# Sliding-window attention and a gated FFN on one core: two weight matrices folded, scores transposed, attention issued in steps between FFN matmuls

## Chip, core, metric

One core of one Trainium2 chip. The metric is the device time of one execution in microseconds. Seven inputs arrive in HBM in fp32, one fp32 output goes back; on the chip the matmul operands are cast to fp16.

## What is computed

```python
# q, k, v: (8 batches, 8 heads, 576 positions, 64), randn * 0.1
scores = q @ k.T / 8, kept where 0 <= i - j < 64, else -1e9
attn   = exp(scores - max); attn = attn / sum(attn)
x      = (attn @ v) as 4608 tokens x 512
# w1, w2: 512 x 1024; w3: 1024 x 1024; w_out: 1024 x 512
out    = ((x @ w1) * (x @ w2)) @ w3 @ w_out
```

## The kernel before

Attention goes over 8 batches and 4 pairs of heads (32 pairs). For a pair, 20 DMAs bring q and k in 128-row pieces and 10 bring v (L99 to L105), all from SyncE's queue (SP); GpSimd (POOL) casts them (L106 to L110); TensorE transposes q and k piece by piece (L116) and ScalarE (ACT) copies each transposed piece out of PSUM (L118). Then each head takes five blocks of 128 (last 64) queries one after the other. A block is a chain: scores for up to 192 keys with queries on the partitions (L128), the mask added by VectorE, DVE (L132), the row maximum (L138), its scaling on ACT (L140), exp with the row sum (L141), the reciprocal on DVE (L145), the division on ACT (L147), one or two transposes of the probabilities (L152, L155) with an ACT copy each (L153, L156), one or two matmuls with v (L157, L160), and an ACT copy into `xT` (L162), which holds the attention's output with the 512 features on partitions.

The FFN goes over 9 groups of 512 tokens. In each group eight column blocks of `a = x@w1` and `b = x@w2` take four matmuls each (L172, L174), ACT copies `a` (L177), DVE multiplies (L178); `g = ab@w3` takes 8x8 matmuls and eight ACT copies (L183, L185); the output takes 4x8 matmuls, four ACT copies and four DMAs (L190, L193, L194). That is 1440 matmuls of 512 columns. Weights are loaded through two fp32 staging buffers and cast by POOL (L75, L76).

The order on each engine is that of the tile scheduler, which takes priorities from the program's order; every engine issues its instructions in order. Four PSUM names (`ps_a` to `ps_d`) with two buffers each serve both parts.

## Time and profile before

| | |
|---|---|
| time, median of 3 runs | 946.75 us (946.46 to 947.27) |
| profiled execution, first to last instruction | 942.8 us |
| busy: TensorE matmul, ACT, DVE, POOL | 689.0, 642.3, 294.3, 99.2 us |
| instructions | 12002 |
| HBM read, written | 39.85 MB, 9.44 MB |

PE is TensorE's matmuls, PEld its weight loads. The profile gives, for each engine, busy time and a strip of 40 slices of the span in tenths; groups of instructions by source line with count, total and mean; the chain of work that ended last; and a timeline. A busy span of a matmul covers its pipeline, so its cost in a stream is the distance from one start to the next, not its own length.

### The profile page before, as it was taken

To read this page: it belongs to the slowest core of one execution; us is meant where nothing else is said; L and a number is where in the kernel's file an instruction comes from. 1 tells how busy PE (TensorE), PEld (TensorE's weight loads), DVE (VectorE), ACT (ScalarE), POOL (GpSimd) and SP (SyncE) were. 2 spreads that over 40 slices of the span, in tenths; PEclk is the share of its full clock that TensorE was granted. 3 is DMA by queue.
4 is the path that set the end of the run, shared out by engine and by line. 5 is a ranking of instruction groups with operands and counts; after the bars stand their busy time and mean duration, and the time that the engine had idled before them with its cause. 6 is when DMAs were issued, how large, how long until landed. Compare 5 with 4: busy or idle time off the path is not lost.

```text
span 942.8 us, 12002 instructions
## 1 busy us (share of the span) xinstructions
PE 689.0 (73%) x3104; PEld 316.8 (34%) x3104; DVE 294.3 (31%) x1033; ACT 642.3 (68%) x2613; POOL 99.2 (11%) x195
## 2 busy tenths in 40 slices
PE   0436666666666666666666666689999999999998
PEld 0212323333232332323232332334444444444443
...
ACT  0649899989998998998999999973333333333332
...
GB/s 216 209 126 61 62 60 60 59 60 61 60 57 54 50 54 47 52 55 45 52 56 51 45 55 8 0 1 12 34 46 22 23 45 34 12 46 45 1 45 45
DMA packets 138757, 50.11 MB, mean 53 GB/s; under 512 B 131008, under 2 KB 131008, under 8 KB 138688
## 3 DMA queue, kind: packets, MB, share of 16 engines
...
q8 instruction: 24, 0.39, 0.2%
...
HBM read 39.85 MB, written 9.44 MB: 52 GB/s over the span
## 4 chain that ended last, share of the span: by engine, by line
PE 46%; ACT 42%; DMA 4%; DVE 3%; issue 3%; POOL 1%; SPq 1%; ACTq 0%; POOLq 0%
PE ps_c L183 13%; ACT sc L141 11%; ACT scp L147 10%; PE ps_b L174 7%; PE ps_a L172 7%; PE ps_d L190 7%; ACT xT L162 7%; ACT at L153 4%; PE ps_a L116 4%; DMA stg<-in_moe_w_dram 4%; ACT at L156 3%; ACT stat L140 3%; ACT qkT L118 3%; PE ps_b L128 3%; PE ps_d L157 2%
## 5 line engine op out<-in xcount | busy, mean ns | idle before, releaser
L152 PE MATMUL ps_c<-ident,scp 128*128 128x128 f16 (+1 forms) x320 | 88.3, 276 | 100.9 <-ACT scp L147 96.2
L141 ACT ACTIVATE sc<-sc,stat 128x192 f32<-128x192 f32 (+2 forms) x320 | 137.8, 431 | 2.6
L147 ACT ACTIVATE scp<-sc,rinv 128x192 f16<-128x192 f32 (+2 forms) x320 | 137.6, 430 | 2.1
L132 DVE TENSOR_TENSOR sc<-ps_b,mask_rest 128x192 f32<-128x192 f32 (+1 forms) x256 | 86.8, 339 | 161.5 <-ACT scp L147 129.8
L183 PE MATMUL ps_c<-ab,w_sb 128*128 128x512 f16 x576 | 125.8, 379 | 0.0
L178 DVE TENSOR_TENSOR ab<-ps_b,a_sb 128x512 f16<-128x512 f32 x72 | 49.8, 692 | 241.1 <-ACT a_sb L177 237.2
L116 PE MATMUL ps_a<-ident,qk 128*128 128x128 f16 (+1 forms) x320 | 76.2, 269 | 55.1 <-POOL qk L106 38.9
L118 ACT COPY qkT<-ps_a 128x128 f16<-128x128 f16 (+1 forms) x320 | 74.9, 256 | 53.1 <-PE ps_a L116 46.9
L172 PE MATMUL ps_a<-xT,w_sb 128*128 128x512 f16 x288 | 109.5, 385 | 0.0
L174 PE MATMUL ps_b<-xT,w_sb 128*128 128x512 f16 x288 | 109.4, 386 | 0.1
L128 PE MATMUL ps_b<-qkT 64*128 64x192 f16 (+2 forms) x320 | 94.8, 309 | 14.2 <-ACT qkT L118 2.5
L138 DVE TENSOR_REDUCE stat<-sc 128x1 f32<-128x192 f32 (+2 forms) x320 | 101.9, 324 | 9.7
L185 ACT CAST gt<-ps_c 128x512 f16<-128x512 f32 x72 | 42.2, 586 | 84.1 <-PE ps_c L183 84.1
L157 PE MATMUL ps_d<-at,v 128*64 128x128 f16 (+1 forms) x320 | 91.6, 287 | 9.7 <-ACT at L153 8.6
L152 PEld LDWEIGHTS <-scp 128*128 128x128 f16 (+1 forms) x320 | 32.9, 103 | 190.7 <-ACT scp L147 189.1
L162 ACT CAST xT<-ps_d 64x128 f16<-64x128 f32 (+1 forms) x320 | 78.2, 245 | 27.6 <-PE ps_d L157 20.1
L177 ACT COPY a_sb<-ps_a 128x512 f32<-128x512 f32 x72 | 42.2, 586 | 76.0 <-PE ps_a L172 76.0
L155 PE MATMUL ps_c<-ident,scp 128*64 128x128 f16 x192 | 53.0, 276 | 48.3 <-ACT at L153 47.4
L153 ACT COPY at<-ps_c 128x128 f16<-128x128 f16 (+1 forms) x320 | 79.8, 250 | 1.9 <-PE ps_c L152 0.6
L145 DVE RECIPROCAL rinv<-stat 128x1 f32<-128x1 f32 (+1 forms) x320 | 50.8, 159 | 93.6 <-ACT sc L141 93.2
L183 PEld LDWEIGHTS <-w_sb 128*128 128x128 f16 x576 | 56.3, 98 | 68.0
L160 PE MATMUL ps_d<-at,v 64*64 64x128 f16 x192 | 54.7, 285 | 21.7 <-ACT at L156 21.7
...
## 6 DMA issues: line engine op xcount, KB each, us to landing
v_stg<-in_v_dram SPq DMA_DIRECT2D x320, 32.0 KB, 1.8
...
qk_stg<-in_q_dram SPq DMA_DIRECT2D x256, 32.0 KB, 1.8
qk_stg<-in_k_dram SPq DMA_DIRECT2D x256, 32.0 KB, 1.8
...
```

Of the source, the lines that this page charges most:

```text
L116: nc.tensor.transpose(tp[:, qk, 0:rows], qk16[0:rows, qk * 640 + t * P:qk * 640 + t * P + P], ident16[0:rows, 0:rows])
L118: nc.scalar.copy(qkT[:, qk, r0:r0 + rows], tp[:, qk, 0:rows])
L128: nc.tensor.matmul(sc_ps[0:rows, 0:nk], qkT[d0:d0 + 64, 0, r0:r0 + rows], qkT[d0:d0 + 64, 1, ks:ks + nk], start=True, stop=True)
L141: nc.scalar.activation(sc[0:rows, 0:nk], sc[0:rows, 0:nk], mybir.ActivationFunctionType.Exp, bias=nmaxs[0:rows], scale=scale, accum_out=rs ...
L147: nc.scalar.mul(scp[0:rows, 0:nk], sc[0:rows, 0:nk], rinv[0:rows])
L152: nc.tensor.transpose(at_ps[:, 0, 0:rows], scp[0:rows, 0:P], ident16[0:rows, 0:rows])
L153: nc.scalar.copy(at[:, 0, 0:rows], at_ps[:, 0, 0:rows])
L157: nc.tensor.matmul(o_ps[:, 0:rows], v16[:, hh, t, :], at[:, 0, 0:rows], start=True, stop=not has_b)
L162: nc.scalar.copy(xT[(h % 2) * 64:(h % 2) * 64 + 64, h // 2, b * S + r0:b * S + r0 + rows], o_ps[:, 0:rows])
L172: nc.tensor.matmul(a_ps, w1_sb[:, dc, fc * P:(fc + 1) * P], xT[:, dc, n0:n0 + NG], start=(dc == 0), stop=(dc == 3))
L174: nc.tensor.matmul(b_ps, w2_sb[:, dc, fc * P:(fc + 1) * P], xT[:, dc, n0:n0 + NG], start=(dc == 0), stop=(dc == 3))
L183: nc.tensor.matmul(g_ps, w3_sb[:, fc, ec * P:(ec + 1) * P], ab[:, fc, :], start=(fc == 0), stop=(fc == 7))
```

## The change

The range-checked softmax needs no row maximum: probabilities are `exp(score/8 - 4)`. Scores are computed with keys on the partitions and two heads in one matmul (q is kept in a tile `qT` that is zero where the other head's features are), so the probabilities need no transpose before the matmul with v. Columns of ones beside v make the same matmul give the row sums. The division is `exp(-ln(sum))` on ACT and a multiplication on DVE. The 576 queries of a pair are three units of 192 (96 units in all); a `tick(u)` issues the scores of unit u, the values of unit u-2, and part of the next pair's transposes, loads or casts. q and k are loaded four heads at a time in two DMAs, v in six.

`w3 @ w_out` is computed on the chip into `wc_sb` (`fold`, eight times), so each FFN group has only `ffn_ab` (8 times) and `ffn_o` (4 times). Under `manual_schedule` the order on each engine is the program's: 14 ticks, then 116 items of FFN work and fold, with one tick after each of the items 0 to 87 but not after items 9, 11, 13 and 15. Four ticks are issued with the eight folds (items 8 to 15), 80 with other items, and 28 items follow without ticks.

The logarithms of the sums go by a small DMA to `lnsum`; at the end a count of rows with `|ln| > 6` is loaded into registers, and only if it is over zero `general_path` runs: a softmax with the row maximum, head by head, as before, then the whole FFN with the folded weights.

```diff
+SEGS = [
+    [(0, 0, 128, True), (64, 128, 64, False)],
+    [(128, 192, 128, False), (256, 256, 128, True)],
+    [(320, 384, 128, False), (448, 448, 128, True)],
+]
+def general_path(tc, q, k, v, out, w1_sb, w2_sb, wc_sb, xT, ident16):
...
-    w3_sb = wpool.tile([P, 8, DF], BF16)
-    wo_sb = wpool.tile([P, 8, DM], BF16)
...
+    fast.enter_context(tc.manual_schedule())
...
+    ps_t = fast.enter_context(tc.tile_pool(name="ps_t", bufs=1, space=PSUM))
+    ps_s = fast.enter_context(tc.tile_pool(name="ps_s", bufs=2, space=PSUM))
+    ps_v = fast.enter_context(tc.tile_pool(name="ps_v", bufs=2, space=PSUM))
+    ps_f = fast.enter_context(tc.tile_pool(name="ps_f", bufs=3, space=PSUM))
+    nc.scalar.preload_act_table_set("natural_log_exp_and_others")
...
+    def load_half(u):
+        b, half = divmod(u, 2)
+        h0 = half * 4
+        q32 = raw.tile([TP, 4, TI * D], FP32, name="q32")
+        k32 = raw.tile([TP, 4, TI * D], FP32, name="k32")
+        v32 = raw.tile([P, 6, 4, D], FP32, name="v32")
+        for t, src in ((k32, k), (q32, q)):
+            nc.sync.dma_start(out=t, in_=src[b, h0:h0 + 4].rearrange("h (p r) d -> p h (r d)", r=TI))
+        for c, s0 in enumerate(VBLK):
+            nc.sync.dma_start(out=v32[:, c], in_=v[b, h0:h0 + 4, s0:s0 + P, :].rearrange("h s d -> s h d"))
+        raws[u] = (q32, k32, v32)
...
+    def cast_half(u, eng_k, eng_q, eng_v):
+        q32, k32, v32 = raws.pop(u)
+        q16 = sb2.tile([TP, TI, 4 * D], FP16, name="q16")
+        k16 = sb2.tile([TP, TI, 4 * D], FP16, name="k16")
+        for t16, t32, cp in ((k16, k32, eng_k), (q16, q32, eng_q)):
+            cp(t16.rearrange("p i (h d) -> p h i d", h=4), t32.rearrange("p h (i d) -> p h i d", d=D))
+        v16 = v16s[u % 3]
+        v4 = v16.rearrange("p c j (a d) -> p (c j) a d", d=D)[:, :, 0:3:2, :]
+        eng_v(v4, v32.rearrange("p c (j a) d -> p (c j) a d", a=2))
...
+    def load_w(dst, src, cp, cols, name="wst"):
+        st = sb3.tile([P, DF], FP32, name=name)
+        nc.sync.dma_start(out=st[:, 0:cols], in_=src)
+        cp(dst, st[:, 0:cols])
...
+    def transpose_k(p):
+        u, jj = divmod(p, 2)
+        q16, k16, v16 = halves[u]
+        kT = sb3.tile([P, S], FP16, name="kT")
+        tp = ps_t.tile([P, TI, TP], FP16, name="tp")
+        for i in range(TI):
+            nc.tensor.transpose(tp[:, i, :], k16[:, i, jj * P:jj * P + P], ident16[0:TP, 0:TP])
+        dve_cp(kT.rearrange("q (p i) -> q p i", i=TI), tp.rearrange("q i p -> q p i"))
+    def transpose_q(p):
+        u, jj = divmod(p, 2)
+        q16, k16, v16 = halves[u]
+        qT = qTs[p % 3]
+        tp = ps_t.tile([P, TI, TP], FP16, name="tp")
+        for i in range(TI):
+            nc.tensor.transpose(tp[:, i, :], q16[:, i, jj * P:jj * P + P], ident16[0:TP, 0:TP])
+        src = tp.rearrange("q i p -> q p i")
+        act_cp(qT[0:D, 0, :].rearrange("q (p i) -> q p i", i=TI), src[0:D])
+        dve_cp(qT[D:P, 1, :].rearrange("q (p i) -> q p i", i=TI), src[D:P])
...
+    def scores(u):
+        p, si = divmod(u, 3)
+        kT, qT = pairs[p]
+        seg = SEGS[si]
+        w = sum(blk[2] for blk in seg)
+        s_ps = ps_s.tile([P, 512], FP32, name="s_ps")
+        c0 = 0
+        for (k0, q0, n, _) in seg:
+            nc.tensor.matmul(s_ps[:, c0:c0 + 2 * n].rearrange("k (a n) -> k a n", a=2), kT[:, k0:k0 + P],
+                             qT[:, :, q0:q0 + n], start=True, stop=True, skip_group_check=True)
+            c0 += 2 * n
+        pt = sb3.tile([P, 512], FP16, name="pt", bufs=4)
+        nc.scalar.activation(pt[:, 0:2 * w], s_ps[:, 0:2 * w], AF.Exp, bias=-SHIFT, scale=scale)
+        nc.vector.tensor_tensor(pt[:, 0:2 * w], pt[:, 0:2 * w], masks[si], ALU.mult)
...
+        o_ps = ps_v.tile([P, 2, 192], FP32, name="o_ps")
+        first = True
+        for a in range(2):
+            c0 = 0
+            for bi, (k0, q0, n, _) in enumerate(seg):
+                nc.tensor.matmul(o_ps[:, a, q0 - q_base:q0 - q_base + n],
+                                 v16[:, si * 2 + bi, jj, a * D:a * D + P],
+                                 pt[:, c0 + a * n:c0 + a * n + n],
+                                 start=first, stop=(bi == 1), skip_group_check=True)
+                first = False
+                c0 += 2 * n
+        if si == 0:
+            lns[p] = sb2.tile([P, S], FP32, name="ln_s")
+        y = lns[p]
+        ys = y[:, q_base:q_base + 192]
+        nc.scalar.activation(ys[0:D], o_ps[D:P, 0, :], AF.Ln)
+        nc.scalar.activation(ys[D:P], o_ps[0:D, 1, :], AF.Ln)
+        r = sb2.tile([P, 192], FP32, name="r")
+        nc.scalar.activation(r, ys, AF.Exp, scale=-1.0)
+        xs = xT[:, j, b * S + q_base:b * S + q_base + 192]
+        nc.vector.tensor_tensor(xs[0:D], o_ps[0:D, 0, :], r[0:D], ALU.mult)
+        nc.vector.tensor_tensor(xs[D:P], o_ps[D:P, 1, :], r[D:P], ALU.mult)
+        if si == 2:
+            nc.sync.dma_start(out=lnsum[2 * p:2 * p + 2, :], in_=y[0:P:D, :])
...
+    def tick(u):
+        if u < NU:
+            scores(u)
+        if 0 <= u - 2 < NU:
+            values(u - 2)
+        p, si = divmod(u, 3)
+        if p + 1 < NP:
+            if si == 0:
+                transpose_k(p + 1)
+            if si == 1:
+                transpose_q(p + 1)
+        if u % 6 == 2:
+            n = u // 6 + 2
+            if n < 2 * B:
+                load_half(n)
+        if u % 6 == 0:
+            n = u // 6 + 1
+            if 1 < n < 2 * B:
+                cast_half(n, pool_cp, pool_cp, pool_cp)
...
+        a_ps = ps_f.tile([P, 512], FP32, name="f_ps")
+        b_ps = ps_f.tile([P, 512], FP32, name="f_ps")
+        for w, d in ((w1_sb, a_ps), (w2_sb, b_ps)):
+            for dc in range(4):
+                nc.tensor.matmul(d, w[:, dc, fc * P:(fc + 1) * P], xs[:, dc, :], start=(dc == 0), stop=(dc == 3))
+        a_sb = sb2.tile([P, 512], FP32, name="a_sb")
+        act_cp(a_sb, a_ps)
+        nc.vector.tensor_tensor(ab[:, fc, :], b_ps, a_sb, ALU.mult)
+    def ffn_o(g, t):
+        ab = abs_[g]
+        o_ps = ps_f.tile([P, 512], FP32, name="f_ps")
+        for fc in range(8):
+            nc.tensor.matmul(o_ps, ab[:, fc, t * P:t * P + P], wc_sb[:, fc, :], start=(fc == 0), stop=(fc == 7))
+        o_sb = sb2.tile([P, 512], FP32, name="o_sb")
+        act_cp(o_sb, o_ps)
+        r0 = g * 512 + t * P
+        nc.sync.dma_start(out=out[r0:r0 + P, :], in_=o_sb)
...
+    def fold(fc):
+        w3 = w3s.pop(fc)
+        tp = ps_t.tile([P, 8, P], FP16, name="tp")
+        for ec in range(8):
+            nc.tensor.transpose(tp[:, ec, :], w3[:, ec * P:(ec + 1) * P], ident16)
+        w3T = sb2.tile([P, 8, P], FP16, name="w3T")
+        dve_cp(w3T, tp)
+        o_ps = ps_f.tile([P, 512], FP32, name="f_ps")
+        for ec in range(8):
+            nc.tensor.matmul(o_ps, w3T[:, ec, :], wo16[:, ec, :], start=(ec == 0), stop=(ec == 7))
+        act_cp(wc_sb[:, fc, :], o_ps)
+        if fc + 2 < 8:
+            load_w3(fc + 2)
...
+    cast_half(0, dve_cp, act_cp, pool_cp)
+    cast_half(1, dve_cp, act_cp, pool_cp)
     for dc in range(4):
+        load_w(w1_sb[:, dc, :], moe_w1[dc * P:(dc + 1) * P, :], dve_cp, DF)
+        load_w(w2_sb[:, dc, :], moe_w2[dc * P:(dc + 1) * P, :], act_cp, DF)
+    transpose_k(0)
+    transpose_q(0)
+    u = 0
+    for _ in range(14):
+        tick(u)
+        u += 1
+    work = []
+    for g in range(N // 512):
+        work += [lambda g=g, fc=fc: ffn_ab(g, fc) for fc in range(8)]
+        if g == 0:
+            work += [lambda fc=fc: fold(fc) for fc in range(8)]
+        work += [lambda g=g, t=t: ffn_o(g, t) for t in range(4)]
+    for i, w in enumerate(work):
+        if i == 2:
+            for ec in range(0, 8, 2):
+                st = sb3.tile([P, DF], FP32, name="wst")
+                nc.sync.dma_start(out=st.rearrange("p (e m) -> p e m", e=2),
+                                  in_=moe_w_out[ec * P:(ec + 2) * P, :].rearrange("(e p) m -> p e m", p=P))
+                pool_cp(wo16[:, ec:ec + 2, :], st.rearrange("p (e m) -> p e m", e=2))
+            load_w3(0)
+            load_w3(1)
+        w()
+        if u < NU + 2 and not (8 <= i < 16 and i % 2):
+            tick(u)
+            u += 1
+    while u < NU + 2:
+        tick(u)
+        u += 1
+    chk = const.tile([2 * NP, S], FP32)
+    nc.vector.tensor_tensor(chk, lnsum, lnsum, ALU.mult)
+    nc.vector.tensor_single_scalar(chk, chk, BOUND * BOUND, op=ALU.is_le)
+    okv = const.tile([2 * NP, 1], FP32)
+    nc.vector.tensor_reduce(okv, chk, axis=mybir.AxisListType.X, op=ALU.min)
+    nc.vector.tensor_scalar(okv, okv, -1.0, 1.0, op0=ALU.mult, op1=ALU.add)
+    ones = const.tile([2 * NP, 1], FP32)
+    nc.vector.memset(ones, 1.0)
+    c_ps = ps_t.tile([1, 1], FP32, name="tp")
+    nc.tensor.matmul(c_ps, okv, ones, start=True, stop=True)
+    nc.vector.tensor_copy(bad_i[0:1, :], c_ps)
+    fast.close()
+    bad = nc.values_load(bad_i[0:1, 0:1], min_val=0, max_val=2 * NP,
+                         skip_runtime_bounds_check_because="a count of 64 flags")
+    with tc.If(bad > 0, preferred_fallthrough_block=False):
+        general_path(tc, q, k, v, out, w1_sb, w2_sb, wc_sb, xT, ident16)
```

## Rows read from the trace of the kernel before

**Rows 1.** The page: busy time of the engines, and the strips of 40 slices.
```profile
PE 689.0 (73%) x3104; PEld 316.8 (34%) x3104; DVE 294.3 (31%) x1033; ACT 642.3 (68%) x2613; POOL 99.2 (11%) x195
PE   0436666666666666666666666689999999999998
ACT  0649899989998998998999999973333333333332
```
**Rows 2.** Busy time by stretch: PE, PEld, DVE, ACT, POOL, granted clock, DMA share, GB/s.
```profile
10.00:20.00 10.00, 0.00 (x0) 0.00 (x0) 0.00 (x0) 0.00 (x0) 4.16 (x4) 1.00 0.79 266
28.00:48.00 20.00, 11.72 (x52) 5.60 (x52) 7.53 (x30) 16.78 (x76) 8.92 (x14) 1.00 0.71 221
130.00:220.00 90.00, 58.06 (x257) 27.25 (x257) 37.39 (x147) 81.74 (x373) 13.63 (x29) 1.00 0.27 60
624.00:630.00 6.00, 4.24 (x15) 1.38 (x15) 2.75 (x11) 4.44 (x21) 0.00 (x0) 0.58 0.00 0
700.00:780.00 80.00, 80.00 (x373) 36.25 (x371) 15.29 (x23) 27.04 (x47) 0.00 (x0) 1.00 0.07 27
```
**Rows 3.** Timeline: first transposes of the attention, first matmul of the FFN.
```profile
28.34 0.39 PE L116 MATMUL ps_a<-ident,qk 128*128 128x128 f16 x2 [28.34 <-POOL qk L106]
613.88 0.61 PE L172 MATMUL ps_a<-xT,w_sb 128*128 128x512 f16 x1
```
**Rows 4.** Timeline: a stream of FFN matmuls; a copy into xT after 613.88.
```profile
641.79 13.98 PE L183 MATMUL ps_c<-ab,w_sb 128*128 128x512 f16 x64
617.22 0.26 ACT L162 CAST xT<-ps_d 64x128 f16<-64x128 f32 x1 [0.44 <-PE ps_d L157]
```
**Rows 5.** Groups by line and shape: ACT and DVE (busy us, mean ns of one).
```profile
L147 ACT ACTIVATE scp<-sc,rinv 128x192 f16<-128x192 f32 x192 | 86.5, 450 | 0.9
L162 ACT CAST xT<-ps_d 64x128 f16<-64x128 f32 x256 | 65.6, 257 | 25.0 <-PE ps_d L157 18.1 <-PE ps_d L160 1.5
L177 ACT COPY a_sb<-ps_a 128x512 f32<-128x512 f32 x72 | 42.2, 586 | 76.0 <-PE ps_a L172 76.0
L185 ACT CAST gt<-ps_c 128x512 f16<-128x512 f32 x72 | 42.2, 586 | 84.1 <-PE ps_c L183 84.1
L132 DVE TENSOR_TENSOR sc<-ps_b,mask_rest 128x192 f32<-128x192 f32 x192 | 68.7, 358 | 124.2 <-ACT scp L147 93.3 <-PE ps_d L160 12.2 <-ACT qkT L118 11.9
L178 DVE TENSOR_TENSOR ab<-ps_b,a_sb 128x512 f16<-128x512 f32 x72 | 49.8, 692 | 241.1 <-ACT a_sb L177 237.2 <-PE ps_b L174 3.9
L76 POOL CAST w_sb<-stg 128x1024 f16<-128x1024 f32 x16 | 16.6, 1039 | 30.1 <-DMA stg<-in_moe_w_dram 30.1
```
**Rows 6.** Timeline: two ACT instructions back to back.
```profile
32.47 0.40 ACT L147 ACTIVATE scp<-sc,rinv 128x128 f16<-128x128 f32 x1
32.77 0.44 ACT L141 ACTIVATE sc<-sc,stat 128x192 f32<-128x192 f32 x1
```
**Rows 7.** Timeline: the same transpose alone in the attention and beside FFN matmuls.
```profile
32.92 0.29 PE L152 MATMUL ps_c<-ident,scp 128*128 128x128 f16 x1 [1.06 <-ACT scp L147]
618.47 0.22 PE L152 MATMUL ps_c<-ident,scp 128*128 128x128 f16 x1
```
**Rows 8.** One line's instructions (min/median/max ns): the FFN's first matmuls.
```profile
L172 PE MATMUL ps_a<-xT,w_sb x288: 379/379/634, 613.9 to 917.6; 128*128 128x512 f16 x144
```
**Rows 9.** Timeline: SP issuing five DMAs of 32 KB, and the first two weight loads.
```profile
300.64 2.25 SPq L105 DMA_DIRECT2D v_stg<-in_v_dram  x5
0.74 0.86 SPq L75 DMA_DIRECT2D stg<-in_moe_w_dram  x2
```
**Rows 10.** Groups by line: the one load of ACT's function table.
```profile
L118 ACT ACT_TABLE_LOAD x1 | 1.3, 1283 | 0.7 <-PEq L209 0.7
```
**Rows 11.** The chain at the end: start us, us, what.
```profile
932.04 6.92 PE ps_d L190 x32
939.02 0.59 ACT o_sb L193
```

More of the change, by code (lines that the diff above doesn't have):

```diff
@@ L72 @@
-    wstg = ctx.enter_context(tc.tile_pool(name="wstg", bufs=2))
-    def _load_w(dst, src):
-        stg = wstg.tile([P, src.shape[1]], FP32)
-        nc.sync.dma_start(out=stg, in_=src)
-        nc.gpsimd.tensor_copy(dst, stg)
-    for dc in range(4):
-        _load_w(w1_sb[:, dc, :], moe_w1[dc * P:(dc + 1) * P, :])
-        _load_w(w2_sb[:, dc, :], moe_w2[dc * P:(dc + 1) * P, :])
-    for fc in range(8):
-        _load_w(w3_sb[:, fc, :], moe_w3[fc * P:(fc + 1) * P, :])
-        _load_w(wo_sb[:, fc, :], moe_w_out[fc * P:(fc + 1) * P, :])
@@ new lines @@
+    scale = 1.0 / (D ** 0.5)
+    NJ = H // 2
+    TP, TI = 96, 6
+    keep = ctx.enter_context(tc.tile_pool(name="keep", bufs=1))
+    ident16 = keep.tile([P, P], FP16)
+    w1_sb = keep.tile([P, 4, DF], FP16)
+    w2_sb = keep.tile([P, 4, DF], FP16)
+    wc_sb = keep.tile([P, 8, DM], FP16)
+    xT = keep.tile([P, NJ, N], FP16)
+    lnsum = keep.tile([2 * B * NJ, S], FP32)
+    bad_i = keep.tile([P, 1], I32)
+    fast = ctx.enter_context(ExitStack())
+    fast.enter_context(tc.manual_schedule())
@@ new lines @@
+    halves = {}
+    v16s = [const.tile([P, 6, 2, 192], FP16, name=f"v16_{i}") for i in range(3)]
+    qTs = [const.tile([P, 2, S], FP16, name=f"qT_{i}") for i in range(3)]
+    def cast_half(u, eng_k, eng_q, eng_v):
[7 more added lines that the diff above has]
+        eng_v(v4, v32.rearrange("p c (j a) d -> p (c j) a d", a=2))
+        halves[u] = (q16, k16, v16)
@@ new lines @@
+    pool_cp = nc.gpsimd.tensor_copy
+    dve_cp = nc.vector.tensor_copy
+    act_cp = nc.scalar.copy
+    load_half(0)
+    load_half(1)
+    make_identity(nc, ident16)
+    masks = []
+    for si, seg in enumerate(SEGS):
+        w = sum(blk[2] for blk in seg)
+        m = const.tile([P, 2 * w], FP16, name=f"mask{si}")
+        nc.gpsimd.memset(m, 1.0)
+        c0 = 0
+        for (_, _, n, first) in seg:
+            sl = m[:, c0:c0 + 2 * n]
+            off = 0 if first else 64
+            nc.gpsimd.affine_select(out=sl, in_=sl, pattern=[[0, 2], [1, n]], compare_op=ALU.is_ge,
+                                    fill=0.0, base=off, channel_multiplier=-1)
+            nc.gpsimd.affine_select(out=sl, in_=sl, pattern=[[0, 2], [-1, n]], compare_op=ALU.is_ge,
+                                    fill=0.0, base=63 - off, channel_multiplier=1)
+            c0 += 2 * n
+        masks.append(m)
@@ new lines, with ffn_ab @@
+    abs_ = {}
+    def ffn_ab(g, fc):
+        if fc == 0:
+            abs_[g] = sb2.tile([P, 8, 512], FP16, name="ab")
+        ab = abs_[g]
+        xs = xT[:, :, g * 512:g * 512 + 512]
+        a_ps = ps_f.tile([P, 512], FP32, name="f_ps")
+        b_ps = ps_f.tile([P, 512], FP32, name="f_ps")
+        for w, d in ((w1_sb, a_ps), (w2_sb, b_ps)):
+            for dc in range(4):
+                nc.tensor.matmul(d, w[:, dc, fc * P:(fc + 1) * P], xs[:, dc, :], start=(dc == 0), stop=(dc == 3))
+        a_sb = sb2.tile([P, 512], FP32, name="a_sb")
+        act_cp(a_sb, a_ps)
+        nc.vector.tensor_tensor(ab[:, fc, :], b_ps, a_sb, ALU.mult)
@@ new lines, in ffn_o, with load_w3 @@
+    def ffn_o(g, t):
+        ab = abs_[g]
+        o_ps = ps_f.tile([P, 512], FP32, name="f_ps")
+        for fc in range(8):
+            nc.tensor.matmul(o_ps, ab[:, fc, t * P:t * P + P], wc_sb[:, fc, :], start=(fc == 0), stop=(fc == 7))
[3 more added lines that the diff above has]
+        nc.sync.dma_start(out=out[r0:r0 + P, :], in_=o_sb)
+    wo16 = const.tile([P, 8, DM], FP16)
+    w3s = {}
+    def load_w3(fc):
+        w3s[fc] = sb2.tile([P, DF], FP16, name="w3_16")
+        load_w(w3s[fc], moe_w3[fc * P:(fc + 1) * P, :], pool_cp, DF)
```

287 lines of the change are left out of this document (141 added, 146 removed).

## Prediction, made before the changed kernel ran

> **What bounds the kernel now.** First the page: its strips show two stages that share almost nothing [rows 1]. In slices 3 to 26 ACT's digits are 8 and 9 while PE's are 6; from slice 28 PE's are 9 and ACT's are 3. So ACT's chain bounds the attention and TensorE the FFN, and each lies half idle while the other works. The stretches say the same in microseconds: from 130 to 220 ACT is busy 81.74 of 90, and PE's 58.06 are lengths of short matmuls, not their spacing; from 700 to 780 PE is busy all the time and ACT 27.04 [rows 2]. The timeline gives the borders: first transposes at 28.34, first FFN matmul at 613.88 [rows 3], so attention has 585.5 us and the FFN, with a little attention left in it, 329 us. In the FFN 64 matmuls of 512 columns take 13.98 us: from start to start (13.98 - 0.38) / 63 = 0.216 us [rows 4]. 1440 of them are 311 us. Two gains are thus open: less work in both stages, and doing one under the other.
>
> **Fold.** The w3 stage loses 576 matmuls x 0.216 = 124 us and 72 ACT copies of 586 ns [rows 5], which had lain beside them. What is left of the FFN is 864 x 0.216 = 187 us: 108 items of eight matmuls, 1.73 us each. The fold adds eight items. One is eight transposes (0.6 us at 0.06 to 0.11 each), a DVE copy of 1024 columns from PSUM, and eight matmuls that need it, 1.73. DVE's price per column from PSUM is (692 - 358) / 320 = 1.04 ns [rows 5], so the copy is about 1.2 us, and TensorE, in order, waits for it with all that is queued behind it (the next tick's scores, the next item). If DVE first has a tick's work to end, the wait is 2 to 3 us; I take 2.0. Eight x 4.35 = 35 us and four ticks' PE work of 0.7 give 38; bounds 30 and 45.
>
> **Attention, ACT.** In place of 76 ACT instructions a pair has 13: exp of 384, 512 and 512 columns from PSUM, six Ln of 192, three exp of 192, one copy of 576. PSUM copies cost 257 ns at 128 columns and 586 at 512, so 147 + 0.857 a column [rows 5]: 476 + 586 + 586 + 9 x 312 + 641 = 5097 ns. With an operand per partition and SBUF as source 192 columns took 450 and not 312 [rows 5]; 138 more on 12 instructions gives 6753. Against that, back to back the second of two starts 0.10 before the first ends (32.47 + 0.40 against 32.77) [rows 6], 1.3 us over 13. A tick, a third of a pair, thus costs ACT between 1.27 and 2.25 us; I take 1.85, nearer the upper end, since the row at 450 is the one that resembles an exp.
>
> **Attention, PE and DVE.** A pair streams 12 x 96 columns of transposes, 1408 of scores (one matmul for two heads, half of whose moving rows are zeros) and 1408 of values, 3968 in all. At 0.216 / 512 a column that is 0.56 us a tick; at the spacing of the first transposes (two in 0.39, each about 0.28, so 0.11 for 128 columns [rows 3]) it is 1.14. The same transpose takes 0.29 in the attention and 0.22 beside FFN matmuls [rows 7]; ticks between FFN items belong to the second case, and I take 0.7. The Trainium skill's page TensorE: Matmul & The Clock Gate (Back-to-back issue gap) gives about 81 ns for each 128-column matmul with its weight load; by that a tick would be an estimated 0.9, and the sum 16 us more. No run here shows it yet. DVE's tick: two copies of 576 columns (2 x 759), three masks (at full price 559 to 692 each), six multiplications of 192 (358 each) over three ticks, at most 1.9 us, with 0.69 for two items of three [rows 5]: 2.3 a step, not the bound. POOL's casts for a half batch, three of 1536 columns at 1039 / 1024 ns [rows 5], are 4.7 us in six ticks: hidden.
>
> **Before the first score.** On DVE the copy of the first kT stands behind casts of k for two halves and of w1, on ACT the first qT behind those of q and w2. So attention waits for all these loads: two halves of 1.97 MB and eight weight rows of 0.52 MB, 8.13 MB. SP's 24 issues at 0.43 to 0.45 us [rows 9] take less than the transfer. At 266 GB/s [rows 2] it is 30.5 us, from 0.74 on; with a cast of 1.04 and the copies the first scores come at 33. At 221 GB/s [rows 2] they come at 41; with the DMA engines full (266 / 0.79 = 337) at 27.
>
> **Fourteen ticks alone.** Nothing lies under them. ACT's 1.85 us, at the 0.91 that it was busy when it was the bound (81.74 of 90 [rows 2]), is 2.03. The transposes have one PSUM buffer (`ps_t`): q's wait for DVE's copy of k's from the tick before, which stands behind that tick's multiplications, and the next scores stand behind them on PE. I add 0.27: 2.3 a tick, 32 us; bounds 25 (ACT without waits) and 45 (3.2, half of each link uncovered). FFN work starts at 65.
>
> **Eighty steps with both.** PE 1.73 + 0.7 = 2.43; ACT 1.85 + 0.586 = 2.44 (each item has one copy of 512 columns); DVE 2.3. Three engines near the same load, in order, each waiting for the others: at 0.91 of the larger, 2.7, and 0.1 for the transposes' buffer: 2.8, so 224 us. Bounds: 2.45 (no waits) and 3.3 (ACT at its upper price, 2.84, at 0.86). That FFN matmuls can start on one part of xT while another is written is in the trace: L172 begins at 613.88, L162 still writes at 617.22 [rows 3, 4]. At the start of FFN work before, matmuls of 512 columns took up to 634 ns instead of 379 [rows 8], and the granted clock of 624 to 630 was 0.58 [rows 2], the lower of two levels, after PE's sparse work; I add 2 us for that once.
>
> **End.** 28 items without ticks: 28 x 1.73 = 48.4. From the last matmul (932.04 + 6.92 = 938.96 [rows 11]) to the end of the span it was 3.84 us: a copy and a DMA; this stays. The flags' vector work runs under the last items, but the count, the register loads and the branch over the general path come last. No row shows such a branch; between 0 and 10 us, I take 3, a few times the 0.7 us that ACT waited at the start for the sequencers [rows 10].
>
> **Sum.** 33 + 32 + 2 + 224 + 38 + 48.4 + 3.8 + 3 = 384.2 for the span. The profiled execution has 942.8, which is 3.95 below the median of 946.75; with the same around it: 388. The bounds taken together on one side would give 330 and 470; not all fall on one side, and this case's own range is 350 to 450.
>
> **Rivals.** (1) No overlap: in-order queues make the steps take turns, PE waiting for ACT's chain of each tick. For it: three engines at the same load and one buffer for transposes. Against it: values are two ticks behind scores, so each wait has a step to end. A step is then 1.73 + 2.3 = 4.03, 80 x 1.23 = 98 more: 486. 7%. (2) TensorE at its lower level under the mixed work, as from 624 to 630 [rows 2]: 0.43 instead of 0.216 for each matmul of 88 items, 8 x 88 x 0.216 = 152 more: 540. Against it: PE has 2.4 of 2.8 us to do, more than in the attention before. 4%. (3) ACT reloads its table when it goes from exp to Ln and back. One load took 1283 ns [rows 10]; two a tick make 2.57, a step 2.57 + 2.44 = 5.0, 80 x 2.2 + 14 x 2.57 + 4 x 2.57 = 222 more: 610. Against it: the program asks for one set with both functions by name, and the trace of before, with exp and copies, has one load. 4%. The Trainium skill's page ScalarE: Activation LUTs (Table sets: the hidden batching unit) says that a change of set costs a load each time and that one set holds both exp and ln; by the latter this case does not occur. (4) The other side: the flags count a row, and the general path runs after all this. It costs about the attention of before, 585 us, and 187 us of FFN: 388 + 772 = 1160. It decides where one of the 36,864 logarithms is over 6 in size. The inputs are 0.1 x normal, so a score has a spread of 0.01 x 8 / 8 = 0.01, and the sums run from one key, e^-4, to 64 keys, 64 e^-4: logarithms from -4.0 to 0.2. 2%.
>
> **How the numbers follow.** Forecast 388, 83%; the rivals 7, 4, 4 and 2%. 350 to 450 leaves out the rivals and little of the forecast's own case. A measurement can tell about 0.2% of this kernel from no change; all cases but (4) are far faster: 0.98 faster, 0 within, 0.02 slower.
>
> **What would show it.** Right: the first scores at 27 to 41; PE's strip 9 from some 65 us on, with ACT at 8 or 9 up to about 330 and 3 after; 2.45 to 3.3 us from one `ffn_ab` to the next; one table load; no instruction of the general path. Wrong: PE idle before L-lines of the values or transposes for over 0.5 us a step (rival 1, or DVE as the bound); matmuls of 512 columns 0.43 apart after 70 us (rival 2); a mean of exp and Ln over 0.75 us, which would make ACT the bound at over 3.3 a step.

## The result, and the profile of the changed kernel

| | before | after |
|---|---|---|
| time, median | 946.39 us | 414.44 us (409.4 to 419.56, 6 runs) |
| ratio | | 0.4339, interval 0.4322 to 0.4357 |
| span of the profiled execution | 942.8 us | 416.3 us |

The profiled execution of after is the longest of its six, 419.56 us, and the ratio rests on the three shortest, whose mean of 410.8 is what gains are reckoned from below. The median lies inside the range of 350 to 450, 26 us above the forecast of 388. The page of after, busy times and strips, answers to [rows 1]; PEclk is the granted clock in tenths:

```profile
PE 299.9 (72%) x1954; PEld 162.7 (39%) x1954; DVE 225.6 (54%) x453; ACT 233.5 (56%) x539; POOL 84.2 (20%) x77
PE   0001657956676695896798689778958899999992
ACT  2132785862220366783888388468839878733331
PEclk9999999996766897999899899969998999999998
DMA  9989077996500093919376673928384520020202
```

The two stages of before now share the engines: from slice 14 to 33 PE's digits are 5 to 9 and ACT's 6 to 9, but for slices 18, 22, 25 and 29, where ACT falls to 3 or 4. In each of these four PE's digit is 5 to 7 and DMA's 6 to 9. Busy time by stretch (columns as in [rows 2]):

```profile
33.00:65.00 32.00, 16.02 (x130) 12.49 (x130) 21.95 (x42) 21.55 (x53) 7.26 (x5) 1.00 0.59 115
65.00:100.00 35.00, 27.27 (x176) 14.62 (x176) 23.51 (x46) 20.15 (x49) 12.86 (x11) 0.90 0.92 219
100.00:140.00 40.00, 24.53 (x134) 12.66 (x133) 11.60 (x21) 10.09 (x24) 9.91 (x9) 0.74 0.18 66
180.00:220.00 40.00, 32.52 (x238) 18.04 (x237) 27.58 (x60) 29.19 (x72) 8.82 (x6) 0.96 0.59 126
```

In the ticks alone (33 to 65) PE is half idle. In the folds (100 to 140) PE has 24.5 of 40 and a granted clock of 0.74. In the mixed steps (180 to 220) PE has 32.5, ACT 29.2 and DVE 27.6 of 40: all wait. The groups by line say for whom (busy us, mean ns, idle before and its releasers):

```profile
L366 PE MATMUL f_ps<-xT,w_sb 128*128 128x512 f16 x576 | 144.8, 399 | 20.2 <-ACT o_sb L377 17.4
L291 DVE TENSOR_TENSOR pt<-pt,mask 128x512 f16<-128x512 f16 (+1 forms) x96 | 51.0, 531 | 63.8 <-ACT pt L290 63.1
L290 ACT ACTIVATE pt<-s_ps 128x512 f16<-128x512 f32 (+1 forms) x96 | 53.9, 562 | 16.2 <-PE s_ps L286 15.8
L270 PE MATMUL tp<-ident,q 96*128 96x96 f16 x192 | 15.1, 222 | 51.2 <-DVE kT L261 51.2
L377 ACT COPY o_sb<-f_ps 128x512 f32<-128x512 f32 x36 | 21.1, 585 | 54.6 <-DMA out_dram<-o_sb 31.7
```

The last row has the new wait. ACT's copy of the FFN output waits 31.7 us for an output DMA to free `o_sb`, in five waits of 6.0 to 6.7 us; PE then waits 17.4 for that copy, because it holds a PSUM buffer, and DVE's masks wait for the exps queued behind it. The timeline has one of the five:

```profile
186.46 6.69 SPq L196 DMA_DIRECT2D v<-in_v_dram  x6
186.47 0.59 ACT L377 COPY o_sb<-f_ps 128x512 f32<-128x512 f32 x1
...
193.25 1.04 SPq L379 DMA_DIRECT2D out_dram<-o_sb  x2
...
198.04 0.58 ACT L377 COPY o_sb<-f_ps 128x512 f32<-128x512 f32 x1 [6.51 <-DMA out_dram<-o_sb]
...
198.68 1.87 PE L366 MATMUL f_ps<-xT,w_sb 128*128 128x512 f16 x4 [3.65 <-ACT o_sb L377]
```

The second output tile of a group is ready at 187.06. Its DMA stands in SP's in-order queue behind six v loads of the next half batch, which SP needs 6.69 us to issue, and leaves at 193.25. The fourth tile needs the second one's buffer, so ACT is held until 198.04. Half batches are loaded every 6 ticks, groups have 12 items, so every second load falls between the first and second `ffn_o` of a group: at 148, 186, 223, 260 and 299 us. The loads delay this output twice. Of ACT's 6.51 us here 1.72 pass before the DMA leaves SP and 4.79 between its issue and the copy; over the five waits it is 10.4 and 21.3 us, or 3.5 to 5.0 from issue to copy, where the median of all output DMAs is 2.3 from issue to landing.

Between the stalls PE runs like this, three steps of one pair of heads:

```profile
204.00 1.89 PE L366 MATMUL f_ps<-xT,w_sb 128*128 128x512 f16 x8
205.73 0.38 PE L286 MATMUL s_ps<-qT,kT 128*128 128x256 f16 x2
205.95 0.33 PE L309 MATMUL o_ps<-pt,v 128*128 128x128 f16 x4
206.12 1.89 PE L366 MATMUL f_ps<-xT,w_sb 128*128 128x512 f16 x8
207.85 0.33 PE L286 MATMUL s_ps<-qT,kT 128*128 128x256 f16 x2
208.01 0.39 PE L309 MATMUL o_ps<-pt,v 128*128 128x128 f16 x4
208.24 0.42 PE L260 MATMUL tp<-ident,k 96*128 96x96 f16 x6
208.49 1.89 PE L366 MATMUL f_ps<-xT,w_sb 128*128 128x512 f16 x8
...
211.38 0.42 PE L270 MATMUL tp<-ident,q 96*128 96x96 f16 x6 [0.56 <-DVE kT L261]
211.63 1.68 PE L366 MATMUL f_ps<-xT,w_sb 128*128 128x512 f16 x7
```

From item to item 2.12, 2.37 and 3.14 us, a mean of 2.54. Eight FFN matmuls are 1.73 of each. Without transposes a tick costs PE 0.39, with k's 0.64; the third step takes 0.77 more than the second, nearly all of it PE's wait for the copy of `kT`, which holds the one `ps_t` buffer (0.56 is counted from the modelled end of the matmul before).

### The profile page after: what moved, and what is told of

Read it like the earlier page. It is cut to its first block, busy times and chain, and to the rows that moved or that the text cites. A ratio compares the mean times of both kernels' runs of the same rounds, so it can differ in the third digit from the quotient of the medians.

```text
span 416.3 us, 5949 instructions
## 1 busy us (share of the span) xinstructions
PE 299.9 (72%) x1954; PEld 162.7 (39%) x1954; DVE 225.6 (54%) x453; ACT 233.5 (56%) x539; POOL 84.2 (20%) x77
## 4 chain that ended last, share of the span: by engine, by line
PE 44%; DVE 13%; SPq 13%; ACT 13%; DMA 9%; issue 5%; ACTq 0%; DVEq 0%
PE f_ps L366 22%; SPq L196 11%; PE f_ps L375 8%; PE f_ps L398 6%; DMA out_dram<-o_sb 5%; DVE kT L261 5%; DMA wst<-in_moe_w_dram 4%; DVE xT L325 3%; PE tp L270 3%; ACT pt L290 2%; ACT ln_s L320 2%; ACT ln_s L319 2%; ACT r L322 2%; DVE pt L291 2%; PE s_ps L286 2%
## 5 line engine op out<-in xcount | busy, mean ns | idle before, releaser
L366 PE MATMUL f_ps<-xT,w_sb 128*128 128x512 f16 x576 | 144.8, 399 | 20.2 <-ACT o_sb L377 17.4
L291 DVE TENSOR_TENSOR pt<-pt,mask 128x512 f16<-128x512 f16 (+1 forms) x96 | 51.0, 531 | 63.8 <-ACT pt L290 63.1
L369 DVE TENSOR_TENSOR ab<-f_ps,a_sb 128x512 f16<-128x512 f32 x72 | 49.8, 691 | 35.2 <-PE f_ps L366 33.5
L375 PE MATMUL f_ps<-wc_sb,ab 128*128 128x512 f16 x288 | 66.6, 379 | 0.0
L290 ACT ACTIVATE pt<-s_ps 128x512 f16<-128x512 f32 (+1 forms) x96 | 53.9, 562 | 16.2 <-PE s_ps L286 15.8
L368 ACT COPY a_sb<-f_ps 128x512 f32<-128x512 f32 x72 | 41.3, 574 | 20.8 <-PE f_ps L366 20.7
L270 PE MATMUL tp<-ident,q 96*128 96x96 f16 x192 | 15.1, 222 | 51.2 <-DVE kT L261 51.2
L377 ACT COPY o_sb<-f_ps 128x512 f32<-128x512 f32 x36 | 21.1, 585 | 54.6 <-DMA out_dram<-o_sb 31.7
L324 DVE TENSOR_TENSOR xT<-o_ps,r 64x192 f16<-64x192 f32 x96 | 33.4, 348 | 31.4 <-ACT r L322 31.1
L286 PE MATMUL s_ps<-qT,kT 128*128 128x256 f16 x192 | 39.0, 289 | 8.9 <-DVE qT L273 8.9
L309 PE MATMUL o_ps<-pt,v 128*128 128x128 f16 (+1 forms) x384 | 38.7, 228 | 0.9 <-ACT pt L290 0.9
L325 DVE TENSOR_TENSOR xT<-o_ps,r 64x192 f16<-64x192 f32 x96 | 34.6, 361 | 1.3
L319 ACT ACTIVATE ln_s<-o_ps 64x192 f32<-64x192 f32 x96 | 31.4, 327 | 3.7 <-PE o_ps L309 1.0
L320 ACT ACTIVATE ln_s<-o_ps 64x192 f32<-64x192 f32 x96 | 30.9, 322 | 1.1
L213 POOL CAST v<-v 128x1536 f16<-128x1536 f32 x16 | 23.6, 1473 | 36.8 <-DMA v<-in_v_dram 34.0
```

Source lines behind the costliest of these rows:

```text
L270: nc.tensor.transpose(tp[:, i, :], q16[:, i, jj * P:jj * P + P], ident16[0:TP, 0:TP])
L286: nc.tensor.matmul(s_ps[:, c0:c0 + 2 * n].rearrange("k (a n) -> k a n", a=2), kT[:, k0:k0 + P], qT[:, :, q0:q0 + n], start=True, stop=True ...
L290: nc.scalar.activation(pt[:, 0:2 * w], s_ps[:, 0:2 * w], AF.Exp, bias=-SHIFT, scale=scale)
L291: nc.vector.tensor_tensor(pt[:, 0:2 * w], pt[:, 0:2 * w], masks[si], ALU.mult)
L309: nc.tensor.matmul(o_ps[:, a, q0 - q_base:q0 - q_base + n], v16[:, si * 2 + bi, jj, a * D:a * D + P], pt[:, c0 + a * n:c0 + a * n + n], st ...
L325: nc.vector.tensor_tensor(xs[D:P], o_ps[D:P, 1, :], r[D:P], ALU.mult)
```

## The experiments

Two families of theories stood against each other. One: the time above the forecast is waits that the order of the program makes (SP's queue, the one buffer for transposes, the fold's copy in line, the weights loaded before the first tick). The other: it is engine time (ACT, DVE or PE full in a step), which no reordering would give back. The last two runs put the pieces together.

**More buffers for the output.** e2 changes nothing but the number of `o_sb` buffers.

```diff
-        o_sb = sb2.tile([P, 512], FP32, name="o_sb")
+        o_sb = sb2.tile([P, 512], FP32, name="o_sb", bufs=5)
```

> o_sb has five buffers instead of two; the DMAs stay in SP's queue behind the v loads. Theory A: four copies of a group find free buffers while the DMA stands in the queue, so nearly the same 25 to 35 us go. If the wait is not for a buffer but for something else that ends at the same time, the time stays at 405 to 418.

Measured: 385.36 us, ratio 0.4076 [0.4059, 0.4093], 25 us below after, the low end of what theory A expected. The group of the copy in e2:

```profile
L377 ACT COPY o_sb<-f_ps 128x512 f32<-128x512 f32 x36 | 21.1, 585 | 27.4 <-PE f_ps L375 27.4
```

No DMA is waited for any more. The 72 mixed steps run from 140.0 to 326.1, 2.58 us each in place of 3.0. So the five stalls cost 25 us between the times compared, and 30 in the profiled execution of after. Not all of the 30 is waiting: in after 39 matmuls of 512 columns run at the lower clock behind the stalls, 8 us in all, and in e2's mixed steps none does.

**The loads moved, two buffers kept.** e5 keeps two buffers and issues a half batch's loads at another tick, three halves ahead; the third half's loads then stand behind the weights, ahead of the first transposes (not shown).

```diff
-        if u % 6 == 2:
-            n = u // 6 + 2
+        if u % 6 == 5:
+            n = u // 6 + 3
```

> Each half batch is loaded with the tick at u % 6 == 5 for the half three ahead, not at u % 6 == 2 for the half two ahead; o_sb keeps two buffers, the queue stays SP. The loads then stand before items 5 and 11 of a group of 12, not before item 8, the first of the four output items. Theory C (phase: six v loads, 6.5 us of SP's queue, fall exactly on the first output DMA): the waits of ACT before o_sb fall from 31.7 us to under 8 and the time by 20 to 32 us, to 382 to 395. Rival B' (the output transfer is slow whenever loads run, whatever their place): under 10 us less.

Measured: 386.05 us, 0.4071 [0.4061, 0.408], the same as e2 within the intervals, and 0.6 us of waiting for output DMAs in place of 31.7. Two cures, one of buffers and one of places, give the same 25 us with the same bytes moved: the loss is that a half's loads meet a group's output DMAs while only two buffers wait for them. Both cures take away the queue's delay and the slow transfer together, so they do not part the two; the next runs do, in part.

**The output on another queue.** e1 issues the output DMA from ACT.

```diff
-        nc.sync.dma_start(out=out[r0:r0 + P, :], in_=o_sb)
+        nc.scalar.dma_start(out=out[r0:r0 + P, :], in_=o_sb)
```

> The 36 output DMAs are issued from ACT's queue instead of SP's; nothing else moves. Theory A (order of SP's queue): in the changed kernel five FFN groups lose about 6.5 us each because the output DMA stands in SP's queue behind six v loads that take about 1.1 us each to issue, ACT's copy into o_sb waits for it, and TensorE waits for ACT. Then the five waits of ACT before o_sb (31.7 us) go, and the time falls by 25 to 35 us to 380 to 390. Rival B (the DMA engines are full in these stretches, the transfer itself is late): the waits stay within a few us and the time stays at 405 to 418.

Measured: 403.88 us, 0.4258 [0.4232, 0.4283]: 7 us, under a third of what e2 gives, and between the two forecasts. The execution that was profiled took 1631.9 us, four times any other, and says nothing of the stalls, so the same kernel was profiled again.

> The same kernel as with output DMAs on ACT's queue and two o_sb buffers, for its profile. It took 404, 10 us less than the changed kernel, where five buffers took 385. If the transfer itself is late (its packets stand behind those of the loads in the DMA engines), ACT still waits 15 to 25 us for the output DMAs before o_sb, with 5 us or more from issue to landing in these places. If the DMA's issue on ACT's queue is the cost instead, the wait for the DMA is under 8 us and ACT is late by its own issues, 0.33 us and more each.

Measured: 406.3 us, one run. Two output tiles in it:

```profile
180.34 0.34 ACTq L379 DMA_DIRECT2D out_dram<-o_sb  x1
180.73 0.60 ACT L290 ACTIVATE pt<-s_ps 128x512 f16<-128x512 f32 x1 [0.42 <-ACT o_sb L377]
...
187.26 0.58 ACT L377 COPY o_sb<-f_ps 128x512 f32<-128x512 f32 x1 [2.40 <-DMA out_dram<-o_sb]
```

ACT stands still 0.42 us around each issue (8.4 us over the 20 before an exp), and still waits for a buffer four times, 9.3 us, between the two cases expected. In this execution SP's order thus accounts for some 22 of the 31.7 us that ACT waited, and the transfer beside the loads for the rest. PE's wait for the copy of `kT` is 64.0 us, 51.2 in after. So the move takes the DMA out of SP's order and charges the busiest in-order chain for it. The tile issued at 180.34 freed its buffer only at 187.26, though the page gives 2.0 us as the median from issue to landing of these DMAs; the DMA share from 180 to 188 is 1.06 to 1.18 with the v loads under way, so the DMA engines were full, but that the tile waited in them is not shown by itself.

**No overlap.** e3 runs all 98 ticks before the FFN.

```diff
-    for _ in range(14):
+    for _ in range(NU + 2):
         tick(u)
```

> All 98 ticks are issued before the first FFN item; the work is the same. If the overlap is worth what was forecast, a tick alone costs 2.2 to 2.3 us and an FFN item 1.73, so 38 for the start, 98 x 2.2 = 216, 108 x 1.73 = 187, folds 35 to 50 and 7 for the end give 480 to 500. If the ticks hide little under the FFN (they take turns), the time stays within 20 us of the changed kernel's 414.

Measured: 457.58 us, 0.4834 [0.4822, 0.4846]. First scores at 38.5, FFN from 235.6: 197.1 / 98 = 2.01 us a tick, less than the 2.2 expected, so the time lies below the 480 to 500. In e3, ticks alone:

```profile
100.00:160.00 60.00, 36.53 (x300) 28.64 (x298) 52.97 (x109) 49.64 (x128) 22.28 (x15) 1.00 0.83 162
```

DVE is busier (53.0 of 60) than ACT (49.6). Issuing the ticks between FFN items is worth 47 us as the change has it, 72 with e2's buffers. The folds, with nothing around them, start 3.13 us apart, 25 us for eight.

**Without the fold's product.** e4 leaves out `w3`: the FFN's output uses `w_out` alone, and the eight folds are gone; every step from item 0 to 83 has a tick.

```diff
-        if g == 0:
-            work += [lambda fc=fc: fold(fc) for fc in range(8)]
...
-            load_w3(0)
-            load_w3(1)
+            nc.gpsimd.tensor_copy(wc_sb, wo16)
```

> Leaves out the product w3 @ w_out: wc_sb is a copy of w_out, w3 is neither loaded nor used, so the output lacks w3; the four ticks that went with folds go with other items. The profile puts items 8 to 15 at 54 us with four ticks in them. If that is the fold's price, 54 less four ticks at 0.7 to 1.0 and a little that moves elsewhere: 42 to 50 us less, 364 to 373. If the forecast's 38 holds (matmuls at full clock, the rest waits for attention that would come anyway), 33 to 37 less, 377 to 381.

Measured: 351.67 us (346.55 to 356.27), some 60 below after, more than either forecast and more than the 53 us that the fold items span. It also shifts the ticks against the groups, so that a half's loads fall elsewhere between the items; ACT's wait for output DMAs is 7.1 us in place of 31.7. The run can't part the two: it leaves the fold's price in place between 25, what the eight take with nothing around them (e3), and 60.

**The fold one step ahead.** e6 adds to e2 that the next block's transposes and copy are issued ahead of this block's matmuls.

```diff
+        if fc + 1 < 8:
+            fold_t(fc + 1)
+        fold_m(fc)
```

> Five buffers for o_sb, and in the fold the transposes of block fc+1 stand on TensorE before the matmuls of block fc. With five buffers alone the time was 385 and the eight folds with their four ticks took about 47 us, their matmuls at 0.43 us apart for much of it. Theory D (TensorE waits for DVE's w3T copy with the next work queued behind it, and the wait lets its clock fall): 10 to 18 us less, 367 to 375, and the matmuls of the fold 379 ns long. Rival E (the folds wait for w3 from HBM and POOL's casts): under 5 us less.

Measured: 369.76 us, 0.3896 [0.3882, 0.391]: 15.6 below e2. The fold's matmuls span 98.1 to 129.6, 31.5 us; in e2 93.2 to 139.8, 46.6. PE's wait for the copy of the transposed block, 0.8 us and more before each of the eight, is mostly gone, and fewer matmuls run at half rate (three groups of eight take over 2.9 us, in e2 five). All of e6's gain lies in the fold.

**The weights behind the first ticks.** e7 adds to e2 that `w1` and `w2` are loaded and cast during ticks 5 to 12.

```diff
     for _ in range(14):
         tick(u)
+        if 5 <= u < 13:
+            w_cast(u - 5)
```

> Five buffers for o_sb; w1 and w2 are cast behind ticks 5 to 12 and loaded behind the third half batch, so the first kT and qT copies no longer stand behind eight weight loads. Theory F (the start is bound by the order of casts on DVE and ACT): first scores at 10 to 14 instead of 38, first FFN matmul at 44 to 50 instead of 64 to 67, 14 to 20 us less: 365 to 371. Rival G (the same 10 MB have to come in before FFN work, and the ticks wait for them): first scores early, but the first FFN matmul at 56 or later and under 9 us less.

Measured: 380.5 us, 0.4015 [0.4005, 0.4026]: first scores at 20.1 in place of 38.3, but the first FFN matmul at 56.0, where e2 has 64.4, and 4.9 us in the end. These are rival G's numbers. SP's queue in e7:

```profile
40.57 7.80 SPq L196 DMA_DIRECT2D v<-in_v_dram  x6
48.47 1.02 SPq L411 DMA_DIRECT2D wst<-in_moe_w_dram  x2
```

The last two weight loads stand behind six v loads: the same order as in the stalls, and PE waits 6.65 us just before 56.0 for DVE, which casts those weights. Of 18 us gained at the scores 8.4 are left at the first FFN matmul and 5.6 at the first fold, before which PE waits 4.78 for POOL's cast of k (2.36 in e2). From 20 to 56 us the DMA share is 0.89, so the transfers may set much of this pace; how much the place of the two loads adds was not tried by itself.

**Transposes ahead of scores.** e8 adds to e2 that a tick issues its transposes first, so the copy of `kT` has a longer time before q's transposes need the buffer.

```diff
+        if p + 1 < NP:
+            if si == 0:
+                transpose_k(p + 1)
+            if si == 1:
+                transpose_q(p + 1)
         if u < NU:
             scores(u)
```

> Five buffers for o_sb; in a tick the transposes come before the scores and values, so DVE's kT copy stands before that tick's mask and multiplications. With five buffers alone TensorE waited 27 us after the start for the kT copy before q's transposes, 0.9 us a pair, and a pair of mixed steps takes 7.6 us. Theory H (the one PSUM buffer for transposes holds TensorE up because the copy stands last on DVE): 10 to 25 us less, 360 to 375. Rival I (DVE is then late with masks and multiplications instead, and the wait moves to the values or to the scores): within 5 us of 385.

Measured: 369.27 us, 0.3903 [0.3888, 0.3918]: 16.1 below e2. In e8:

```profile
L270 PE MATMUL tp<-ident,q 96*128 96x96 f16 x192 | 14.9, 220 | 36.9 <-DVE kT L261 36.7
```

24.8 us of it are the wait for the weights at the start; the rest is 12 us in place of 28 in e2. The mixed steps come to (311.9 - 138.1) / 72 = 2.41 us.

**The fold in the old kernel.** e9 is the kernel before with `w3 @ w_out` multiplied on the chip ahead of the FFN, and nothing else.

```diff
+    for fc in range(8):
...
+        for ec in range(8):
+            nc.tensor.matmul(c_ps, w3T[:, ec, :], wo_sb[:, ec, :], start=(ec == 0), stop=(ec == 7))
+        nc.scalar.copy(wc_sb[:, fc, :], c_ps)
...
-nc.tensor.matmul(o_ps[0:tn, :], gt[:, ec, ts:ts + tn], wo_sb[:, ec, :],
+nc.tensor.matmul(o_ps[0:tn, :], ab[:, ec, ts:ts + tn], wc_sb[:, ec, :],
```

> The kernel before with one part of the change alone: w3 @ w_out is computed on the chip before the FFN, the w3 stage goes, attention stays as it was. By the sum of the prediction 576 matmuls x 0.216 = 124 us go and eight folds of 1.7 to 4.4 us come, 14 to 35 us, some of them under the attention: 835 to 865. The rest of the way from 946 to 414 is then the new attention and its place between FFN matmuls. If the w3 stage had been partly hidden, or the fold costs as much as in the changed kernel without being hidden (63 us), 880 or more.

Measured: 844.83 us, 0.8921 [0.889, 0.8952], 102 below, inside the 835 to 865 expected: the 124 us of 576 matmuls less what the fold adds. The rest of the way came with the rewritten attention and its interleaving: 387 us to e3, which has the one without the other, and 47 from there.

**All of it.** e11 joins e2, e5, e6 and e8 with an earlier start: the first ticks wait for the first half batch alone, the second half is cast after tick 1, the weights come during ticks 5 to 12.

```diff
     cast_half(0, dve_cp, act_cp, pool_cp)
-    cast_half(1, dve_cp, act_cp, pool_cp)
     transpose_k(0)
     transpose_q(0)
+    load_half(2)
...
         tick(u)
+        if u == 1:
+            cast_half(1, dve_cp, act_cp, pool_cp)
+        if 5 <= u < 13:
+            w_cast(u - 5)
+        if u == 10:
+            load_half(3)
```

> All that helped, together: five o_sb buffers, half batches loaded at u % 6 == 5, fold transposes one block ahead, transposes first in a tick, and a start in which the first pair's transposes and the first ticks come before the casts of w1, w2 and of the second half batch; the fourth half batch is loaded only after the last weights. If the gains add up: 385 less 15.6 (fold) less 16 (transposes first) less 15 to 20 (start: first scores at 11 to 14, FFN from 46 to 50) is 333 to 340. If the DMA engines bound the first 130 us (41.9 MB read, over half of it needed before the last fold; above 250 GB/s in the full slices), the start gives 5 or less and the sum ends at 345 to 355.

Measured: 348.0 us, 0.3668 [0.3648, 0.3688], inside the second case by its number. But the start did give what the first case wanted, first scores at 12.4 and the first FFN matmul at 46.7; the gain was lost behind it. PE's two longest waits after that, in e11:

```profile
79.09 0.66 PE L260 MATMUL tp<-ident,k 96*128 96x96 f16 x6 [6.73 <-POOL k L210]
108.73 1.04 PE L394 MATMUL tp<-ident,w 128*128 128x128 f16 x8 [6.92 <-POOL w L249]
```

Both wait for a cast on POOL, and POOL in all 23.2 us for rows of `w3` to land and 40.6 for k. In the stretches 0 to 12.4, 12.4 to 46.7 and 46.7 to 70 us the DMA share is 0.97, 1.00 and 1.07, so up to there the transfers probably set the pace; what holds up the rows of `w3` after it was not tried.

**POOL's casts in pieces.** e12 cuts the casts of e11 into four (k, q) and three (v) instructions.

```diff
-            cp(t16.rearrange("p i (h d) -> p h i d", h=4), t32.rearrange("p h (i d) -> p h i d", d=D))
+            for h in range(4):
+                cp(t16[:, :, h * D:(h + 1) * D], t32[:, h].rearrange("p (i d) -> p i d", d=D))
```

> e11 with POOL's casts cut into pieces: k and q of a head in four pieces of 384 columns each, v in three, in place of one instruction of 1.47 us; the same work otherwise. Theory (a cast that runs on POOL holds up the mask multiplication on VectorE for as long as it lasts): the mask multiplication, 588 ns in the mean and up to 1.7 us in e11, comes to about 430 ns with none over 0.8, and the time to 333 to 345 us, 3 to 15 below e11. Rival (the long multiplications have another cause, or the cover of the FFN matmuls takes them anyway): mean still above 550 ns, or the time within 3 us of 348; if POOL's fixed cost of an instruction decides, POOL's busy time grows by over 15 us and the time is above 351.

Measured: 339.31 us, 0.3593 [0.3578, 0.3608], inside the theory's range. The mask multiplication in e12:

```profile
L293 DVE TENSOR_TENSOR pt<-pt,mask x96: 348/426/3121, 13.2 to 277.7; 128x512 f16<-128x512 f16 x64, 128x384 f16<-128x384 f16 x32
```

The mean went from 588 to 517 ns, not to 430. Seven are over 0.8 us, 20 in e11, and one, at 113.46, took 3.12 while casts of q and then of v ran on POOL without a gap. POOL's busy time grew by 17.7 us (84.1 to 101.8), as the rival feared, but the time fell all the same. The theory holds in direction and in the time; that pieces free DVE altogether does not. From the fold's end to the last values e12 needs 167.0 us, e11 172.9: 5.9 of the 9.8 us between the two profiled spans (346.3 and 336.5) lie in the mixed steps. At 2.32 us a step little but PE's own time is left: 2.12, 2.37 and, without its wait, 2.43 in the three steps above, a mean of 2.31. PE is busy nearly all the time in e12 (columns as before):

```profile
220.00:280.00 60.00, 59.88 (x451) 34.08 (x450) 52.21 (x112) 56.57 (x141) 12.21 (x23) 1.00 0.44 102
```

So the first family of theories held for the mixed steps: the changes of order took a step from 3.0 us to 2.40 (e11), the cut casts took another 0.08, and PE's own time is left.

## Why the prediction came out as it did

| term of the sum | forecast, us | profiled execution |
|---|---|---|
| to the first scores | 33 | 38.3 |
| fourteen ticks alone | 32 | 28.9 |
| items 0 to 7 with ticks, and the 2 us of low clock | 24.4 | 23.6 |
| folds with four ticks | 38 | 53.2 |
| 72 steps with both | 201.6 | 216.4 |
| 28 items | 48.4 | 48.4 |
| from there to the end | 6.8 | 7.5 |
| span | 384.2 | 416.3 |

The mechanism was right: two stages that left each other's engine idle now lie over each other, both with less work. Two terms make 30 of the 32 us above the forecast in this execution, the longest; the start's 5.3 and the ticks' -3.1 partly balance. The bounds of the terms add up, with the 3.95 around the span, to 336 and 463 and not to the 330 and 470 named; the range does not hang on this.

**The mixed steps: a term was missing.** The prediction built 2.8 us from three in-order engines and a transposes' buffer, and counted SP's issues only for the start, at the 0.43 to 0.45 us of [rows 9]. In the steps six v loads hold SP for 6.5 to 7.8 us, 1.1 and more each, and output DMAs stand behind them. Between the stalls a step takes 2.54 to 2.58, so 0.2 less than forecast; the stalls put 0.4 on. That 2.8 lay near 3.0 is luck: one error on each side. The prediction asked what frees the transposes' PSUM buffer, but not what frees `o_sb`, which was the one that mattered.

**The engines' prices were near.** A pair costs ACT 2 x 598 + 490 (exp) + 3 x (327 + 322) (Ln) + 3 x 363 (exp of the negative) + 620 = 5342 ns, 1.78 a tick against 1.85. The 1.85 was chosen between two corrections that did not come: an exp of 512 columns takes 598 and not 138 more than a copy's 586, and instructions back to back do not overlap (one of 0.33 starts at 187.47, the next at 187.81). DVE's copies of 576 columns took 757 (759 forecast). PE's tick is 0.39, 0.64 and, with q's transposes and without its wait, 0.70, a mean of 0.58 us, near the 0.56 that the columns gave and not 0.7: in a stream of FFN matmuls the short ones run at nearly their columns' price. By the 81 ns for a 128-column matmul that the Trainium skill's page TensorE: Matmul & The Clock Gate (Back-to-back issue gap) gives, a tick would have been an estimated 0.9; the four value matmuls that start at 208.01 and give way at 208.24, 57 ns each, and the six transposes after them, 0.25 to the next start, do not agree with it. Alone, DVE is busier in a tick than ACT (53.0 and 49.6 of 60 us in e3).

**The fold: mis-sized.** The copy itself is cheaper than the forecast had it: DVE needs 0.69 us, not 1.2, and PE waits 0.79. What was not in the sum is seen here, two folds of after:

```profile
126.89 1.01 PE L393 MATMUL tp<-ident,w 128*128 128x128 f16 x8 [3.00 <-DVE kT L261]
128.69 3.59 PE L398 MATMUL f_ps<-wo,w3T 128*128 128x512 f16 x8 [0.79 <-DVE w3T L395]
132.07 1.06 PE L393 MATMUL tp<-ident,w 128*128 128x128 f16 x8
133.92 1.90 PE L398 MATMUL f_ps<-wo,w3T 128*128 128x512 f16 x8 [0.79 <-DVE w3T L395]
```

First, the fold's transposes share `ps_t` with the tick's, so after each of the four sets of k's or q's transposes PE waits for their copy, and once for the fold's own copy behind the tick's work on DVE: 2.6 to 3.0 us, five times, 14.3 in all. With seven waits of 0.79 that is 19.8 where the forecast had 16. Second, in six of the eight groups of matmuls, wholly or in part, they start 0.42 apart: 3.38 from 128.69 to 132.07 where eight at the higher level are 1.73. The excess over the eight folds is 8.7 us. The two make 12.5 of the 15.2 above the forecast; transposes at the lower level (1.01 in place of 0.61) take most of the rest. The granted clock of 100 to 140 is 0.74, between the two levels of 1.2 and 2.4 GHz, after PE's waits. This is rival 2 in the folds. It comes back in the mixed steps for a few us behind each of the five stalls, after PE has waited 3.1 to 3.8 us, and not in e2, which has no stalls (rows of after, then of e2):

```profile
270.00:282.00 12.00, 8.51 (x39) 4.06 (x39) 6.98 (x15) 8.08 (x19) 1.47 (x1) 0.72 0.31 95
277.66 3.14 PE L366 MATMUL f_ps<-xT,w_sb 128*128 128x512 f16 x8
141.00:326.00 185.00, 167.17 (x1266) 95.45 (x1265) 146.03 (x303) 156.35 (x377) 44.15 (x30) 1.00 0.64 142
```

Without ticks between them the eight take 25 us (e3), and pipelined 31.5 (e6).

**The start.** The last row of `w2` came at 35.9, not at 31.3. SP issues the third half's loads from 28.84, so they share the DMA engines with the last weights; that this is the 4.6 us is argued and not shown by a run. The first scores came 2.4 us after it, where the sum left 1.7:

```profile
35.89 1.04 ACT L249 CAST w_sb<-wst 128x1024 f16<-128x1024 f32 x1 [5.84 <-DMA wst<-in_moe_w_dram]
...
38.32 0.48 PE L286 MATMUL s_ps<-qT,kT 128*128 128x256 f16 x2 [5.84 <-DVE qT L273]
```

**The other rivals.** Rival 1, no overlap, did not come, and e3 shows that its 486 was too high: without any overlap the time is 457.6, as a tick alone is 2.01 and not 2.3. Rival 3 did not come: there is one table load, 1283 ns, at 0.80 us, with 192 Ln and 192 exp behind it. This agrees with what the Trainium skill's page ScalarE: Activation LUTs (Table sets: the hidden batching unit) states, that one set holds both functions. Rival 4 did not come: no instruction of the general path ran, and the end took 7.5 us where 6.8 were forecast.

**The signs named beforehand.** First scores, step, table load and general path came as the sign for right had them. PE's strip at 9 from 65 us on, with ACT at 8 or 9, did not: the stalls and the folds break both. Of the signs for wrong, matmuls 0.43 apart came in part, in the folds and behind the stalls.
